# Block 1's second product as seven half products, with its inputs ahead of most of w2

## The chip, the core and the metric

The kernel runs on one core of one Trainium2 chip. TensorE (PE in the profile, its weight loads PEld) multiplies, VectorE (DVE), ScalarE (ACT) and GpSimd (POOL) do the rest, and SyncE (SP), POOL and ACT issue the transfers. Each engine takes its instructions in the order in which they were written. The metric is the device time of one execution in microseconds.

## What is computed

There are 8 batches of 576 rows, and 8 heads of 64. Per head, `kv = k^T v` and `out = q kv`. Each row of each head is divided by its root mean square and multiplied by `g_norm`. The heads side by side give `x` (576 rows of 512). The second part is a layer with a residual:

```
xn  = (x - mean(x)) / sqrt(var(x) + 1e-6) * g_ln
out = x + relu(xn @ w_ch1) @ w_ch2        # w_ch1: 512 x 2048, w_ch2: 2048 x 512
```

The kernel scales the rows by the reciprocal of the standard deviation (`rstd`) only when the second product is evicted, since that factor passes through the relu.

## The kernel before

**Blocks.** Rows are worked through in blocks of 512, in four tiles of 128: one block for each batch (0 to 7), and a last one, "rem", of the 64 rows that each batch has left. A block has a first product (`mm1`, line 665, matmuls of line 675, evicted with a relu by ACT at line 678 into `m1`) and a second product. The first product is made for 1, 2 or 4 tiles at a time (matmuls of 128, 256 or 512 columns): one tile at a time in blocks 0 and 1, two in block 2, four behind it.

**The second product.** Blocks 0 and 1 make it directly: 64 matmuls of 512 columns each (line 697), evicted by `finish` (lines 702 to 708) with one DVE instruction per tile, which scales by `rstd` and adds `x`. The blocks in `SEVEN` (line 481) cut the product into 2 x 2 quarters and make it with seven half-size products instead of eight (`mm2_seven`, lines 539 to 600): 7 x 16 matmuls of 256 columns (line 519). The price is sums: T1 to T4 of the quarters of w2, made once (lines 494 to 497, 1.2 us each on DVE), and S1 to S4 of the quarters of `m1`, made for each block by DVE (`row_sums`, lines 499 to 511) while the first product still runs. p1 to p7 are evicted by ACT (line 553) or DVE (line 558), and POOL makes the remaining additions (lines 570 to 592). In block 2 the order is p1, p4, p2, p5, p6, p7, p3.

**A tile of x.** `plan_tile` (line 451) sets out the steps. First: `o` (four matmuls, line 298), its squares on ACT (304), their sum on DVE (`red`, 375). Two slots later: the root on ACT (383), and on DVE the reciprocal, y, x, the mean and the centred rows xc (390 to 422). Then the turn of xc into `xT_blk`, which the first product reads: on PE in block 1 (429, copied by ACT at 431), and by a transposing DMA from SP (433) from block 2 on. The variance (415) can come later. `kv_of` (264) makes kv of a batch, 40 small matmuls on PE and two casts on ACT. q is turned by `turn_q_dma` (217): a DVE copy and one long transposing DMA on SP; for batch 1 by `q_start` (884) and `q_turns` (892), two of five parts on PE.

**The order of the work** is written out by hand. PE's stream of products counts ticks (`tick`, line 757): a first product has 16, a direct second product 16, the seven products 14. `at(slot, fn)` (line 748) puts work in front of the matmuls of a tick. A slot is written as 32 x block + r; where the block is in `SEVEN`, what lies in its second half is squeezed:

```python
        if r > 16 and i < len(blocks) and blocks[int(i)] in SEVEN:
            r = 16 + (r - 16) * 14 / 16
        s = sum(30 if x in SEVEN else 32 for x in blocks[:int(i)]) + r
```

So tick 32 is the start of block 1 and tick 48 that of its second product; block 2 begins at tick 64. Work of one tick goes to its engines in the order of the slots, and row sums go ahead of it.

**Loads.** All loads from DRAM are issued by POOL, in order, and cast to bf16 on the way: batch 0, w1, then lines 172 to 178 (w2 in five parts, with q, k, v of batch 1 between them), then one batch after the other (`load_batches`, line 100). The later ones wait behind a tiny copy (`gate`, line 105) of what must have landed first. There are two buffers for q, k and v.

Of the kernel before, what the change touches and what calls it, by code (L numbers as in the profile page):

```python
# [14 lines left out]
def kernel(  # L15
# [11 lines left out]
    nc = tc.nc  # L27
# [142 lines left out]
        nc.vector.memset(t, 0.0)  # L170

    load_w2(0, 4)
    load_w2(4, 8)
    for dst, src in ((q_in, q), (k_in, k), (v_in, v)):
        load(dst[1], src, 1)
    load_w2(8, 10)
    load_w2(10, 12)
    load_w2(12, nDe)
# [299 lines left out]

    SEVEN = {2, 3, 4, 5, 6, 7, "rem"}
    H2, C2 = nDe // 2, Dm // 2
    SPLIT = (0, 6, 12, nDe)
    SPLIT_2, TICKS_2 = (0, 12, nDe), ((0, 1, 4, 7), (0, 1, 4, 6))
# [5 lines left out]
    def w2_q(odd, cols):  # L490
        return w2_sb[:, odd::2, cols * C2:cols * C2 + C2]

    B11, B12, B21, B22 = (w2_q(o, c) for o, c in ((0, 0), (0, 1), (1, 0), (1, 1)))
    weight_sums = (lambda: nc.vector.tensor_sub(T1, B12, B11),
                   lambda: nc.vector.tensor_sub(T3, B22, B12),
                   lambda: nc.vector.tensor_add(T2, T3, B11),
                   lambda: nc.vector.tensor_sub(T4, B21, T2))

    def row_sums(b, i0, i1, ticks):
        if b not in sums:  # L500
# [38 lines left out]
    def mm2_seven(b):  # L539
        V, G = nc.vector, nc.gpsimd  # L540
        S1, S2, S3, S4 = sums.pop(b)
        a11, a12, a22 = m1_q(b, 0, 0), m1_q(b, 0, 1), m1_q(b, 1, 1)
        b11, b21, b22 = w2_q(0, 0), w2_q(1, 0), w2_q(1, 1)
        x, o, o_sb = outs(b)
        p_x, p_q = half(ps1, "p1", "p_x"), half(ps1, "p1", "p_q")
        p_y, p_z = half(ps2, "p2", "p_y"), half(ps2, "p2", "p_z")
        v0, v1, r5, u2, u3, q = (half(fpool, n, n) for n in ("v0", "v1", "r5", "u2", "u3", "q"))
        rstd = rstds[b]

        def scaled(dst, src, rows):  # L550

            for t in range(2):
                nc.scalar.activation(dst[:, t], src[:, t], func=AF.Copy,  # L553
                                     scale=rstd[:, 2 * rows + t:2 * rows + t + 1])

        def scaled_add(dst, src, rows, other):
            for t in range(2):
                V.scalar_tensor_tensor(dst[:, t], in0=src[:, t],  # L558
                                       scalar=rstd[:, 2 * rows + t:2 * rows + t + 1],
                                       in1=other[:, t], op0=ALU.mult, op1=ALU.add)  # L560

        def p1():
            product(p_x, a11, b11, True, False)
            scaled(v0, p_x, 0)
            scaled(v1, p_x, 1)

        def p2():
            product(p_x, a12, b21, False, True)
            scaled(o(0, 0), p_x, 0)
            G.tensor_add(o(0, 0), o(0, 0), x(0, 0))  # L570

        def p3():
            product(p_y, S3, T3, False, True)
            scaled_add(u3, p_y, 1, v1)
            G.tensor_add(o(1, 0), u3, q)
            G.tensor_add(o(1, 1), u3, r5)
            store(b, 2, o_sb[1])

        def p4():
            product(p_q, a22, T4, True, True)  # L580
            scaled(q, p_q, 1)
            G.tensor_add(q, q, x(1, 0))  # L582

        def p5():
            product(p_z, S1, T1, True, False)
            scaled(r5, p_z, 1)
            G.tensor_add(r5, r5, x(1, 1))

        def p6():
            product(p_y, S2, T2, True, False)  # L590
            scaled_add(u2, p_y, 0, v0)
            G.tensor_add(u2, u2, x(0, 1))

        def p7():
            product(p_z, S4, b22, False, True)
            scaled_add(o(0, 1), p_z, 0, u2)
            store(b, 0, o_sb[0])

        for p in ((p1, p4, p2, p5, p6, p7, p3) if b == 2 else (p1, p4, p6, p5, p2, p3, p7)):
            p()  # L600

    def mm2_seven_last(b):
# [62 lines left out]
    def mm1(b, t0, n, c0=0, c1=nDe):  # L665
# [3 lines left out]
        for de0 in range(c0, c1, per):  # L669
            tick()  # L670
            p1 = ps1.tile([128, per, n * 128], f32, tag="p1", name="p1")
            for i in range(per):
                de = de0 + i
                for kk in range(nK):
                    nc.tensor.matmul(p1[:, i, :], lhsT=w1_sb[:, kk, de * 128:(de + 1) * 128],  # L675
                                     rhs=blk[2][:, kk, sl],
                                     start=(kk == 0), stop=(kk == nK - 1))
            nc.scalar.activation(m1[:, de0:de0 + per, sl], p1, func=AF.Relu)  # L678
            del p1
            if b == 2 and t0 + n == 4 and de0 + per in SPLIT_2:  # L680
                i = SPLIT_2.index(de0 + per)
                row_sums(b, SPLIT_2[i - 1] // 2, SPLIT_2[i] // 2, TICKS_2[i - 1])
            elif b in SEVEN and b != 2 and de0 + 1 in SPLIT:
                i = SPLIT.index(de0 + 1)
                row_sums(b, SPLIT[i - 1] // 2, SPLIT[i] // 2, range(4))

# [15 lines left out]
    def finish(b, ts, p2):  # L702
        if ts % 2 == 0:
            o_pair[b] = outp.tile([128, 2, Dm], f32, tag="osb", name="o_sb")
        o_sb = o_pair[b][:, ts % 2]
        nc.vector.scalar_tensor_tensor(o_sb, in0=p2, scalar=rstds[b][:, ts:ts + 1],
                                       in1=blks[b][0][:, ts], op0=ALU.mult, op1=ALU.add)
        store(b, ts, o_pair[b][:, ts % 2:ts % 2 + 1])

    def store(b, ts, o_sb, c0=0, c1=Dm, upper=None):  # L710
# [163 lines left out]
    at(5, lambda: t[2].turn(True))  # L874
    at(5.1, before_5)
    at(9.5, next_memsets)
    load_batches(9.6, (("k", 2), ("v", 2), ("q", 2)), lambda: ())
    at(11, lambda: t[3].turn(True))
    for i in range(4):
        at(16 + i, lambda i=i: t[i].var())  # L880
# [13 lines left out]
        turn_q(1, 1, ps_m, "misc")  # L894
        del q_ps[1]

    at(14.5, q_start)
    at(19, q_turns)
    at(23, lambda: kv_of(1))
    for j, s, tn in ((0, 24, 30), (1, 27, 34), (2, 31, 38), (3, 35, 42)):  # L900
        plan_tile(s, lambda j=j: main_tile(1, j), tn, True, s + 6.7)
    at(36.2, lambda: keep_q(1))
    at(46, lambda: rstd_of(1))

    at(36, lambda: kv_of(2))
    at(36.9, lambda: turn_q_dma(2))
    for j, s, tn in ((0, 45, 51), (1, 49, 55), (2, 53, 61), (3, 57.5, 63)):
        plan_tile(s, lambda j=j: main_tile(2, j), tn, False, s + 6.7)
    at(58, lambda: keep_q(2))
    at(70, lambda: rstd_of(2))  # L910


    def turned_q(b):
        return (qts[b][:1, J, HP - 1, 127:] if b in qts else qj[:1, b, HP - 1, 63:])

    for slot, what, after in (
            (47, (("k", 3), ("v", 3), ("q", 3)), lambda: (turned_q(2),)),
            (68, (("q", 4), ("k", 4), ("v", 4)),
             lambda: (turned_q(3), blks[2][2][:1, nK - 1, 511:])),
            (92.7, (("q", 5), ("k", 5), ("v", 5)), lambda: (turned_q(4),)),  # L920
# [2 lines left out]
        load_batches(slot, what, after)  # L923


    for b, s in ((3, 56), (4, 93), (5, 123), (6, 155), (7, 187)):
        at(s, lambda b=b: kv_of(b))
    rems = {}

# [84 lines left out]
```

## Time and profile before

| what | value |
|---|---|
| median of 3 runs | 279.48 us (279.31 to 280.29) |
| the profiled execution | 279.33 us, span 277.3 us |
| PE busy | 269.2 us, 97% of the span, granted clock 1.0 |
| DVE, ACT, POOL busy | 195.9, 179.5, 101.7 us |
| block 0's second product starts on PE | 32.44 us |
| block 1's first product, second product | from 48.48 us, from 64.89 us |
| block 2's first product, second product | from 80.23 us, from 95.14 us |
| block 3 starts | 109.20 us |
| DMA engines | full from about 6 us to about 55 us, some 200 GB/s |
| last part of w2: issued, landed | 30.26 us, 43.67 us |
| q, k, v of batch 1 landed | 31.19, 34.11, 37.31 us |

The times in the rows are counted from the first instruction. The span is a little shorter than the execution's own time, which is the one that is compared. A view in order of time has the start, the length, the engine, the line, the operation, what it writes and reads, the count, and in square brackets the idle time ahead of it with what ended it. "Landed" is when the semaphore of a transfer showed it as complete.

### The profile page before, as it was taken

The page shows a single profiled execution, that of the slowest core. Times are in us where ns is not written, and L with a number is a line of the kernel's source. Part 1 is how long each engine was busy: PE and PEld are TensorE (multiplying, and loading weights), DVE is VectorE, ACT ScalarE, POOL GpSimd, SP SyncE. Part 2 cuts the span into 40 slices and gives each one's busy share as a digit, 9 for nine tenths or more (in the row PEclk, how much of TensorE's full clock was granted, in tenths as well). Part 3 has the DMA queues.
Part 4 walks back from the last instruction along what each step waited for, and adds up shares of the span by engine and source line. Part 5 has one row for each costly group of instructions (what it writes and reads, how often), then busy time and mean ns, then how long its engine had stood idle before and what let it go on. Part 6 is the DMA issues. An engine that isn't in the chain of part 4 may idle for free.

```text
span 277.3 us, 6629 instructions
## 1 busy us (share of the span) xinstructions
PE 269.2 (97%) x2614; PEld 189.6 (68%) x2614; DVE 195.9 (71%) x446; ACT 179.5 (65%) x398; POOL 101.7 (37%) x127
## 2 busy tenths in 40 slices
PE   8899999999999999999999999999999999999994
PEld 3589855996569886458845874597458745874683
DVE  6676438897966898899569856985797469923564
ACT  3567754796448783777677767776777487846610
POOL 8522770025034256701870187017201800180141
PEclk9999999999999999999999999999999999999999
DMA  7999999959995994995499639991611061105032
GB/s 215 199 207 205 200 197 190 260 106 144 189 183 84 199 126 92 216 227 98 41 185 239 134 26 178 245 134 21 161 28 21 20 163 29 21 20 151 2 76 76
DMA packets 65366, 36.80 MB, mean 133 GB/s; under 512 B 35120, under 2 KB 62004, under 8 KB 65336
## 3 DMA queue, kind: packets, MB, share of 16 engines
q0 software_dynamic: 28736, 18.29, 46.4%
q1 hardware_dynamic: 36008, 17.12, 30.4%
q10 hardware_dynamic: 592, 0.98, 1.0%
q8 instruction: 20, 0.33, 0.5%
q14 instruction: 10, 0.08, 0.1%
HBM read 36.71 MB, written 9.44 MB: 166 GB/s over the span
## 4 chain that ended last, share of the span: by engine, by line
PE 82%; DVE 8%; DMA 4%; ACT 3%; issue 1%; POOL 1%; DVEq 0%; POOLq 0%
PE p L675 42%; PE p L697 8%; PE p_y L519 7%; PE p_z L519 7%; PE p_x L519 6%; PE p_s L519 4%; DMA w_sb<-in_moe_w_ch_dram 4%; PE p_q L519 3%; PE o_ps L298 2%; PE kv_ps L271 2%; DVE S L509 1%; DVE ss L375 1%; DVE x_blk L397 1%; DVE o_ps L379 1%; DVE S L508 1%
## 5 line engine op out<-in xcount | busy, mean ns | idle before, releaser
L675 PE MATMUL p<-xT_blk,w_sb 128*128 128x128 bf16 (+2 forms) x1024 | 131.5, 286 | 0.6 <-DMA w_sb<-in_moe_w_ch_dram 0.4
L678 ACT ACTIVATE m<-p 128x512 bf16<-128x512 f32 x144 | 85.5, 597 | 38.9 <-PE p L675 36.2
L675 PEld LDWEIGHTS <-w_sb 128*128 128x128 bf16 x1024 | 78.7, 98 | 45.0 <-issue 0.7
L519 PEld LDWEIGHTS <-m 128*128 128x128 bf16 x448 | 43.3, 98 | 6.5
L375 DVE TENSOR_REDUCE ss<-sq 128x8 f32<-128x512 f32 x35 | 23.8, 680 | 28.7 <-ACT sq L304 28.6
L582 POOL TENSOR_TENSOR q<-q,x_blk 128x512 f32<-128x512 f32 x6 | 8.1, 1348 | 83.1 <-ACT q L553 83.1
L519 PEld LDWEIGHTS <-S 128*128 128x128 bf16 x344 | 32.8, 98 | 4.8 <-DVE S L509 1.1
L697 PE MATMUL p<-w_sb,m 128*128 128x512 bf16 x128 | 29.6, 379 | 0.0
L415 ACT ACTIVATE dev<-x_blk,st_blk 128x512 f32<-128x512 f32 x36 | 25.8, 718 | 1.4 <-DVE st_blk L401 1.4
L379 DVE TENSOR_TENSOR o_ps<-o_ps,inv 128x512 f32<-128x512 f32 x33 | 23.1, 700 | 3.1
L304 ACT ACTIVATE sq<-o_ps 128x512 f32<-128x512 f32 x35 | 20.8, 595 | 5.0 <-PE o_ps L298 5.0
L397 DVE SCALAR_TENSOR_TENSOR x_blk<-o_ps,g_norm_sb 128x512 f32<-128x512 f32 x33 | 22.8, 691 | 1.1
L519 PE MATMUL p_x<-w_sb,m 128*128 128x256 bf16 x192 | 23.4, 273 | 0.0
L697 PEld LDWEIGHTS <-m 128*128 128x128 bf16 x128 | 12.0, 98 | 12.3
L383 ACT ACTIVATE rms<-ss,eps_sb 128x8 f32<-128x8 f32 x36 | 10.7, 297 | 12.6 <-DVE ss L375 12.2
L507 DVE TENSOR_TENSOR S<-m 128x768 bf16<-128x768 bf16 (+2 forms) x20 | 10.7, 536 | 11.4 <-ACT m L678 11.4
L422 DVE TENSOR_SCALAR xc<-x_blk,st_blk 128x512 bf16<-128x512 f32 x32 | 17.7, 553 | 1.1
L558 DVE SCALAR_TENSOR_TENSOR u<-p_y,rstd,v 128x256 f32<-128x256 f32 x24 | 10.4, 476 | 5.0 <-PE p_y L519 5.0
L509 DVE TENSOR_TENSOR S<-m,S 128x768 bf16<-128x768 bf16 (+2 forms) x20 | 12.6, 634 | 0.4
L553 ACT ACTIVATE v<-p_x,rstd 128x256 f32<-128x256 f32 x24 | 9.4, 475 | 5.0 <-PE p_x L519 5.0
L390 DVE RECIPROCAL inv<-rms 128x8 f32<-128x8 f32 x36 | 7.1, 197 | 7.6 <-ACT rms L383 7.3
L519 PE MATMUL p_z<-w_sb,S 128*128 128x256 bf16 x96 | 11.8, 273 | 0.6 <-DVE S L509 0.6
(143 smaller groups left out, 347.6 us busy)
## 6 DMA issues: line engine op xcount, KB each, us to landing
out_dram<-o_sb SPq DMA_DIRECT2D x24, 256.0 KB, 6.1
w_sb<-in_moe_w_ch_dram POOLq DMA_DIRECT2D x7, 512.0 KB, 13.5
q_in<-in_q_dram POOLq DMA_DIRECT2D x7, 320.0 KB, 5.2
k_in<-in_k_dram POOLq DMA_DIRECT2D x7, 320.0 KB, 7.8
v_in<-in_v_dram POOLq DMA_DIRECT2D x7, 320.0 KB, 11.1
q_in<-in_q_dram POOLq DMA_DIRECT2D x8, 256.0 KB, 8.2
out_dram<-o_sb SPq DMA_DIRECT2D x16, 128.0 KB, 4.6
k_in<-in_k_dram POOLq DMA_DIRECT2D x7, 256.0 KB, 8.7
```

The costliest lines, as they stand in the source:

```text
L304: nc.scalar.activation(self.sq_t, self.o_ps, func=AF.Square)
L375: nc.vector.tensor_reduce(self.ss, self.sq_t, axis=AX.X, op=ALU.add)
L379: nc.vector.tensor_mul(self.o_ps, self.o_ps, self.inv().to_broadcast([128, H, D]))
L383: nc.scalar.activation(self.r, self.ss, func=AF.Sqrt, scale=1.0 / D, bias=eps_sb)
L397: nc.vector.scalar_tensor_tensor(x_blk[:, ts].rearrange("p (h d) -> p h d", h=H), in0=self.o_ps, scalar=1.0, in1=g_norm_sb.to_broadcast([1 ...
L415: nc.scalar.activation(dev, x_blk[:, ts], func=AF.Square, bias=st[:, 1, ts:ts + 1], accum_out=st[:, 2, ts:ts + 1])
L422: nc.vector.tensor_scalar_add(self.xc_t, x_blk[:, self.ts], st[:, 1, self.ts:self.ts + 1])
L509: lambda: nc.vector.tensor_sub(S4, a12, S2),
L519: nc.tensor.matmul(dst[:, t - ts[0], :c1 - c0], lhsT=a[:, i, t * 128:(t + 1) * 128], rhs=w[:, i, c0:c1], start=start and t == ts[0] and i ...
L675: nc.tensor.matmul(p1[:, i, :], lhsT=w1_sb[:, kk, de * 128:(de + 1) * 128], rhs=blk[2][:, kk, sl], start=(kk == 0), stop=(kk == nK - 1))
L678: nc.scalar.activation(m1[:, de0:de0 + per, sl], p1, func=AF.Relu)
L697: nc.tensor.matmul(p2[:, c0:c1], lhsT=m1s[b][:, de, ts * 128:(ts + 1) * 128], rhs=w2_sb[:, de, c0:c1], start=(de == 0), stop=(de == nDe - 1))
```

## The change

Block 1 joins `SEVEN`, so that it makes its second product with seven half products, in block 2's order. The block then has 30 ticks: block 2 begins at tick 62, and everything behind it counts two ticks less. What goes with it:

- The loads of q, k and v of batch 1 are issued ahead of w2's rows 4 to 8 (of 16), which are cut in two. Block 0's second product is cut to match.
- The weight sums are made in four pieces of two slices, the first at slot 13, and the rest at 34.5, 37 and 39.
- In blocks 1 and 2 three of POOL's additions (`o(0,0)`, `q`, `r5`) are put off until p6 has been evicted.
- `finish` of tiles 0 and 1 (block 0 alone uses it now) scales on ACT and adds on POOL.
- Block 1's first product is made for two tiles at a time.
- Batch 1's steps come two to four slots earlier. Batch 2's tiles, its kv and its q get new slots, some of which lie around the row sums of block 1, and so do those of batch 3. Batches 2 and 3 load q first.

```diff
     load_w2(0, 4)
-    load_w2(4, 8)
     for dst, src in ((q_in, q), (k_in, k), (v_in, v)):
         load(dst[1], src, 1)
+    load_w2(4, 6)
+    load_w2(6, 8)
     load_w2(8, 10)
...
-    SEVEN = {2, 3, 4, 5, 6, 7, "rem"}
+    SEVEN = {1, 2, 3, 4, 5, 6, 7, "rem"}
...
-    weight_sums = (lambda: nc.vector.tensor_sub(T1, B12, B11),
-                   lambda: nc.vector.tensor_sub(T3, B22, B12),
-                   lambda: nc.vector.tensor_add(T2, T3, B11),
-                   lambda: nc.vector.tensor_sub(T4, B21, T2))
+    def weight_sums(i0, i1):
+        i = slice(i0, i1)
+        t1, t2, t3, t4, b11, b12, b21, b22 = (w[:, i] for w in (T1, T2, T3, T4, B11, B12, B21, B22))
+        nc.vector.tensor_sub(t3, b22, b12)
+        nc.vector.tensor_add(t2, t3, b11)
+        nc.vector.tensor_sub(t4, b21, t2)
+        nc.vector.tensor_sub(t1, b12, b11)
...
+        late = []
+        def add(dst, a, c):
+            if b in (1, 2):
+                late.append(lambda: G.tensor_add(dst, a, c))
+            else:
+                G.tensor_add(dst, a, c)
...
-            G.tensor_add(o(0, 0), o(0, 0), x(0, 0))
+            add(o(0, 0), o(0, 0), x(0, 0))
...
-            G.tensor_add(q, q, x(1, 0))
+            add(q, q, x(1, 0))
...
-            G.tensor_add(r5, r5, x(1, 1))
+            add(r5, r5, x(1, 1))
...
             G.tensor_add(u2, u2, x(0, 1))
+            while late:
+                late.pop(1 if len(late) == 3 else 0)()
...
-        for p in ((p1, p4, p2, p5, p6, p7, p3) if b == 2 else (p1, p4, p6, p5, p2, p3, p7)):
+        for p in ((p1, p4, p2, p5, p6, p7, p3) if b in (1, 2) else (p1, p4, p6, p5, p2, p3, p7)):
...
-            if b == 2 and t0 + n == 4 and de0 + per in SPLIT_2:
+            if b in (1, 2) and t0 + n == 4 and de0 + per in SPLIT_2:
...
+        if ts < 2:
+            nc.scalar.activation(o_sb, p2, func=AF.Copy, scale=r)
+            nc.gpsimd.tensor_add(o_sb, o_sb, x)
+        else:
+            nc.vector.scalar_tensor_tensor(o_sb, in0=p2, scalar=r, in1=x,
+                                           op0=ALU.mult, op1=ALU.add)
...
-    load_batches(9.6, (("k", 2), ("v", 2), ("q", 2)), lambda: ())
+    load_batches(9.6, (("q", 2), ("k", 2), ("v", 2)), lambda: ())
...
-    at(14.5, q_start)
-    at(19, q_turns)
-    at(23, lambda: kv_of(1))
-    for j, s, tn in ((0, 24, 30), (1, 27, 34), (2, 31, 38), (3, 35, 42)):
-        plan_tile(s, lambda j=j: main_tile(1, j), tn, True, s + 6.7)
-    at(36.2, lambda: keep_q(1))
+    at(12.5, q_start)
+    at(17, q_turns)
+    at(20, lambda: kv_of(1))
+    for j, s, tn in ((0, 21, 27), (1, 24, 31), (2, 28, 35), (3, 31.5, 38)):
+        plan_tile(s, lambda j=j: main_tile(1, j), tn, True, (27.7, 33, 41, 44.5)[j])
+    at(33.2, lambda: keep_q(1))
...
-    at(36, lambda: kv_of(2))
-    at(36.9, lambda: turn_q_dma(2))
-    for j, s, tn in ((0, 45, 51), (1, 49, 55), (2, 53, 61), (3, 57.5, 63)):
-        plan_tile(s, lambda j=j: main_tile(2, j), tn, False, s + 6.7)
-    at(58, lambda: keep_q(2))
-    at(70, lambda: rstd_of(2))
+    at(40, lambda: kv_of(2))
+    at(34, lambda: turn_q_dma(2))
+    for j, s, tn in ((0, 43.2, 48), (1, 48.3, 53.5), (2, 58.3, 61.5), (3, 63.3, 67.5)):
+        plan_tile(s, lambda j=j: main_tile(2, j), tn, False, (55.5, 59.5, 63, 67.5)[j])
+    at(64, lambda: keep_q(2))
+    at(70.5, lambda: rstd_of(2))
...
-            (47, (("k", 3), ("v", 3), ("q", 3)), lambda: (turned_q(2),)),
+            (43, (("q", 3), ("k", 3), ("v", 3)), lambda: (turned_q(2),)),
...
-    for b, s in ((3, 56), (4, 93), (5, 123), (6, 155), (7, 187)):
+    for b, s in ((3, 60), (4, 93), (5, 123), (6, 155), (7, 187)):
...
-    for b, at_q, at_o in ((3, 56.2, (66.9, 70.7, 74.5, 78.4)), (4, 81, (96.5, 102.7, 109, 115)),
+    for b, at_q, at_o in ((3, 52.7, (68.5, 72.5, 76.5, 83)), (4, 81, (96.5, 102.7, 109, 115)),
...
-    for i, fn in enumerate(weight_sums):
-        at(40 + i, fn)
+    for i0, i1, slot in ((0, 2, 13), (2, 4, 34.5), (4, 6, 37), (6, 8, 39)):
+        at(slot, lambda i0=i0, i1=i1: weight_sums(i0, i1))
...
-    for de0, de1 in ((0, 8), (8, 10), (10, 12)):
+    for de0, de1 in ((0, 4), (4, 6), (6, 8), (8, 10), (10, 12)):
...
-    for ts in range(4):
-        mm1(1, ts, 1)
+    mm1(1, 0, 2)
+    mm1(1, 2, 2)
     mm2(1)
```

More of the change, by code (lines that the diff above doesn't have):

```diff
@@ L679, in mm1 @@
             del p1
-            if b == 2 and t0 + n == 4 and de0 + per in SPLIT_2:
+            if b in (1, 2) and t0 + n == 4 and de0 + per in SPLIT_2:
                 i = SPLIT_2.index(de0 + per)
                 row_sums(b, SPLIT_2[i - 1] // 2, SPLIT_2[i] // 2, TICKS_2[i - 1])
-            elif b in SEVEN and b != 2 and de0 + 1 in SPLIT:
+            elif b in SEVEN and b not in (1, 2) and de0 + 1 in SPLIT:
                 i = SPLIT.index(de0 + 1)
@@ L705, in finish @@
         o_sb = o_pair[b][:, ts % 2]
-        nc.vector.scalar_tensor_tensor(o_sb, in0=p2, scalar=rstds[b][:, ts:ts + 1],
-                                       in1=blks[b][0][:, ts], op0=ALU.mult, op1=ALU.add)
+        r, x = rstds[b][:, ts:ts + 1], blks[b][0][:, ts]
+        if ts < 2:
[4 more added lines that the diff above has]
+                                           op0=ALU.mult, op1=ALU.add)
         store(b, ts, o_pair[b][:, ts % 2:ts % 2 + 1])
```

## The prediction

> **What bounds the kernel now.** First the page's shares by engine, then the chain that ended last, then PE's waits, then DVE, ACT, POOL and SP in order of time between 28 and 110 us, then the DMA issues with their landings.
>
> ```profile
> PE 269.2 (97%) x2614; PEld 189.6 (68%) x2614; DVE 195.9 (71%) x446; ACT 179.5 (65%) x398; POOL 101.7 (37%) x127
> PEclk9999999999999999999999999999999999999999
> ```
>
> TensorE is busy 97% of the span at a full granted clock. What the other engines do counts only where TensorE waits for it. The chain gives the pace of each kind of product:
>
> ```profile
> 55.67 3.57 PE p L675 x64
> 66.14 3.45 PE p L697 x16
> 82.41 3.49 PE p L675 x32
> 123.85 1.75 PE p_x L519 x16
> ```
>
> The columns are start, length, line, count: 55.8 ns for 128 columns (first product, tile by tile), 215.7 for 512 (direct second product), 109.1 for 256 (first product by two tiles, 3.49/32) and 109.2 (seven-product form). Waits of PE:
>
> ```profile
> PE p L675 <- DMA w_sb<-in_moe_w_ch_dram: 0.4, 1, 0.4
> PE p_z L519 <- DVE S L509: 0.6, 1, 0.6
> ```
>
> Few are named, since most gaps are shorter than the list counts. I therefore add up PE's work from 32.44 us (block 0's second product starts) to 109.20 (block 3 starts), 76.76 us. Two direct second products 2 x 64 x 0.2157 = 27.60; the first product of block 1, 256 x 0.0558 = 14.28, and of block 2, 128 x 0.1091 = 13.97; the seven products of block 2, 7 x 1.747 = 12.23; turning q 0.45; four kv_of at 0.75 = 3.00; 16 groups of four matmuls (12 `o`, 4 turns) at 0.22 = 3.52. Sum 75.05, so 1.71 us are waits, about one of them in block 2's p7, where the lines below show why.
>
> ```profile
> 101.75 1.44 POOL L570 TENSOR_TENSOR o_sb<-o_sb,x_blk 128x512 f32<-128x512 f32 x1
> 101.99 3.42 DVE L509 TENSOR_TENSOR S<-m,S 128x1536 bf16<-128x1536 bf16 x2
> ```
>
> These are the timelines of POOL and DVE. The pair L509 takes 3.42 us, where a 128x1536 sum at 94.81 takes 0.95 and a 128x512 one 0.42: while POOL adds, such DVE instructions take turns with it.
>
> **The products.** Block 1's 64 matmuls of 13.80 us become 112 of 12.23: -1.57. Its first product by two tiles, 14.28 to 13.97: -0.31. No copies are added on PE. From block 3 on everything is PE-bound and unchanged, so what is won by 109 us is won at the end.
>
> [...]
>
> **The old waits.** At most 1.71 us go. Block 2's `q`, `o(0,0)` and `r5` adds now come after p6, so its S4 no longer alternates with them; and with finish(0) halved on DVE the rest of the small gaps may close. So the bound is 3.59 us (1.57 + 0.31 + 1.71), less whatever is late next.
>
> **Block 0, slots 12 to 31.** POOL's loads keep coming out of one full pipe, and the next is issued when an earlier one has landed:
>
> ```profile
> 30.26 0.76 POOL L119 DMA_DIRECT2D w_sb<-in_moe_w_ch_dram  x1 [1.11 <-DMA q_in<-in_q_dram]
> 33.66 4.37 SPq L888 DMA_TRANSPOSE qt<-q_p  x1
> ```
>
> Today w2(4,8) lands at 28.16, 2.5 us after w2(0,4), then q at 31.19, k at 34.11, v at 37.31, the last w2 at 43.67. Moved, q lands near 28.7 and v near 34.8; both halves of w2(4,8) follow. DVE copies q at 28.7 (0.82 as at 55.11, no memset on POOL yet, against 2.35 beside memsets), so SP issues L888 at 29.6, not 33.66. Landing 13.36 later as now: 43.0; bounds 4.9 (an undisturbed one, 56.09) and the old landing of 47.02. It moves 393 KB in 48 us summed over 16 engines, 3 us of the whole pipe, and now all of it lies ahead of the last w2: that comes 1.0 later, at 44.7. By adding PE's ticks: kv_of(1) at 36.4 needs v (35.1 with the transposition's share), w2(4,6) is needed at 37.1 (36.8), w2(6,8) at 39 (38.5), the rest of q at 44.7 (43.0), w2(12,16) at 45.0 (44.7). Nothing is late, by 0.3 at the closest. I take 0.1 for this and for tile 3's turn at tick 38, whose xc ends at 54.4 as PE arrives. The one extra DMA issue on POOL (0.75, w2(4,8) in two) hides in POOL's waits (1.1 to 1.9). The two finish(0) on ACT (0.6 each) and POOL (1.3 each) relieve DVE of 1.3; their stores leave some 1.5 later, and nobody waits. The sixteen small weight sums are 4 x 1.22 = 4.9 plus some 0.5 for the cut. A quarter runs at 29.5, where DVE waits for PE now, the rest by 59.4, ahead of p4 at 66.
>
> What stands behind the moved waits: behind the copy of q on DVE (slot 12.5) only the first weight sums and the scaling of w1, which waits for PE until 32.5 anyhow; behind `keep_q(1)` on POOL the gate copy of batch 3's loads, which itself waits for batch 2's q (its transposition issued at 55.1, landed near 60, as 60.95 now); behind the root of tile 3 on ACT (slot 33.5, free at 51.4 when its red is done) one eviction of the first product, due at 50.7 and done by 52.2, and PE, with three buffers, asks for that buffer at 52.6. Batch 2's loads end near 55.0 as now (55.03, the same bytes), with v in place of q as the last; kv_of(2) at slot 40 comes at 56.3. If that cover of 1.3 were gone, PE would wait one for one.
>
> **Batch 2's tiles and block 1's row sums.** T is the start of tick 43: 32.44 + 13.80 + 0.45 + 2 kv_of 1.50 + 8 groups 1.76 + 11 ticks of 0.873 = 59.6, with the 0.1 59.7. From T, PE reaches block 2's first half (tick 62) at 5 x 0.873 + 12.23 + 4 x 0.22 + 0.75 = 18.23. DVE, by its rows: red 1.15 to 1.75, second tile step 2.87 to 5.25 (82.14 to 87.38 in block 2 now), S1 and S2 of the first 12 (0.87 each) to 7.05, S1's rest 0.33, red of tile 1 0.60, S2's rest 0.33, S4 0.87 to 9.2, second step of tile 1 2.36 to 11.56, S4's rest 0.33, copy of q3 0.75 to 12.65. All sums precede their products (S1 at 10.1, S2 11.8, S4 13.8, S3 16.3). But SP first gets batch 3's q (slot 52.7), then tile 1's transposition (53.5):
>
> ```profile
> 76.92 3.17 SPq L224 DMA_TRANSPOSE qt<-q_p  x1
> 127.39 3.05 SPq L224 DMA_TRANSPOSE qt<-q_p  x1
> 130.49 3.38 SPq L433 DMA_TRANSPOSE xT_blk<-xc  x2
> ```
>
> q occupies SP for 3.1, so tile 1 is issued at T + 15.85. Such transpositions land after 2.4 to 8.6 us; 3.13 (131.96, no load or store beside it) is nearest, as batch 3's loads end near 74.5 and block 1's stores have not begun. Landed at T + 18.98: a new wait of 0.75.
>
> Then tile 3. Its `o` is at tick 61, T + 17.14. DVE is behind: S3 to 13.85, red 14.45, u2 15.3, tile 2's step from 15.7, whose xc waits for POOL's add and ends at 18.3; o(0,1) 19.15, red 19.75, u3 20.6. ACT's root stands behind the eviction of tick 62, at T + 20.7; tile 3's step starts at 21.0, its xc meets POOL's five adds (1.25 each, from 15.35) and is done at 23.8. Transposed:
>
> ```profile
> xT_blk<-xc SPq DMA_TRANSPOSE x1, 3.5
> ```
>
> That is the transposition of 80.14, beside block 1's stores as here; the next one took 4.00. T + 27.3. PE wants it at 18.98 + 8 x 0.873 + 0.22 = 26.2: another 1.1. Bounds of the two waits together: 0, and 6.2 at 8.6 us of landing. Block 2 behind it: batch 3's last tile is now at slot 83, its xc near 103, landed near 107 for 107.4; no wait, by 0.5.
>
> **Sum.** -3.59 + 0.1 + 0.75 + 1.1 = -1.6. The profiled execution took 279.33, its span 277.3; the median of the three is 279.48, 0.15 above. 279.33 - 1.6 + 0.15 = 277.9.
>
> **Rivals.** A, the forecast: 277.9, its own range 277.2 to 278.8 (landings of 2.4 to 4.4). B, the transpositions come in time: S sums and tiles run ahead of my DVE walk, since in the trace DVE has gaps of up to 3 us in this form of block (132.7 to 135.8); against it, SP's order is fixed. Then -3.5, 276.0. C, block 0 starves: the half of q that SP turns lands at the old 47.0 and PE waits 2.4 at tick 28, or w2 comes by as much later; for it, a pipe that is full from 4 to 55 us and margins of 0.3; against it, the bytes ahead of the last w2 are the same. 280.3. D, slower: tile 3's transposition, behind block 1's 512 KB store on the same SP queue and beside POOL's 512 KB, takes 7.5 to 8.6 as at 67.61, 91.44 and 116.70. 277.9 + 4.0 to 5.1, 281.9 to 283.0; the gain is gone at a landing of 5.1, and the kernel is slower by over 0.5% from 6.5. Against it: those three lay among POOL's loads, and batch 4's loads here wait for this very tile (the gate copy of line 105).
>
> **Chances.** A 0.44, B 0.25, C 0.16, D 0.15. About 0.5% (1.4 us, so 278.1 and 280.9) is what a measurement of this kernel can tell from no change. Of A 0.27 lies below 278.1 and 0.17 within; B is faster; of C 0.02 faster, 0.12 the same, 0.02 slower; of D 0.04 the same, 0.11 slower. Faster 0.54, same 0.33, slower 0.13. The range reaches to B and C, 276.0 to 280.3, and leaves out D's upper part and little of B.
>
> **What the profile after would show.** Sixteen matmuls of L519 in 1.75 us for block 1; L697 with 64 matmuls; block 1's second product starting near 64.4 and block 3 near 107.6, against 109.2. PE waiting for a DMA into xT_blk twice, near 78 and 86, 0.7 to 1.1 each; none for w2; none for S in block 2. The two finish steps on ACT near 46. A wait for w_sb or qt between 36 and 46 makes C right; a wait over 3 us at 86 makes D right.

## The result and the profile after

The changed kernel takes 283.66 us (median of 6 executions, 283.23 to 285.37), the kernel before 279.45 on the same chip. The ratio is 1.0154, with a 95% interval of 1.0127 to 1.0182: slower by 1.5%, where 277.9 was predicted and 276.0 to 280.3 was the range.

The profiled execution of the kernel after took 285.37 us, its span 283.4. It is the slowest of the six, for a reason that its clock row shows. These are the shares by engine and the granted clock, from the page of the kernel after:

```profile
PE 270.2 (95%) x2518; PEld 193.5 (68%) x2534; DVE 198.7 (70%) x466; ACT 184.6 (65%) x410; POOL 109.8 (39%) x134
PEclk9999999999999799999999999999999999999999
```

TensorE's share falls from 97% to 95%, and one slice in 40, near 95 us, has a granted clock of 0.7. PE's waits, in the same columns as before (who waits for whom, sum, times, longest):

```profile
PE p L690 <- DMA xT_blk<-xc: 2.7, 2, 2.0
PE o_ps L299 <- DMA qt<-q_p: 1.8, 1, 1.8
...
PE p L712 <- DMA w_sb<-in_moe_w_ch_dram: 0.8, 2, 0.4
PE p_y L523 <- DVE S L512: 0.6, 1, 0.6
```

The list counts idle time only. I count a wait as the distance from one matmul's start to the next, less the pace of its kind, which makes each 0.1 to 0.2 us longer. So counted, the kernel before has two waits of 0.15 us or more behind 30 us, 0.23 at 52.73 (`kv_of(2)`) and 0.74 at 105.47 (p7 for S), and the kernel after has seven. The chain that ended last passes through most of them (start, length, what):

```profile
30.71 15.32 DMA w_sb<-in_moe_w_ch_dram
...
56.45 6.59 DMA qt<-q_p
...
76.42 3.19 SPq L225
79.65 2.70 DMA xT_blk<-xc
82.39 1.05 PE p L690 x8
...
86.87 5.00 DMA xT_blk<-xc
92.01 5.32 PE p L690 x32
...
97.55 3.49 PE p L690 x32
```

| place | wait | PE waits for |
|---|---|---|
| 37.74 | 0.59 | w2's rows 4 to 6, landed 37.70 |
| 46.08 | 0.54 | w2's last rows, landed 46.03 (43.67 before) |
| 55.62 | 0.18 | xc of batch 1's tile 3 |
| 63.08 | 2.00 | batch 2's turned q, for `o` of its first tile |
| 82.39 | 0.84 | batch 2's tile 1 turned by SP |
| 92.01 | 2.18 | batch 2's tile 3 turned by SP |
| 133.76 | 0.72 | S of block 3, for its third product |

Together 7.05. The windows view shows what came with the last but one (window, us, PE busy, PEld, DVE, ACT, POOL, then granted clock, DMA share, GB/s):

```profile
90.00:92.00 2.00, 0.00 (x0) 0.03 (x1) 1.90 (x6) 0.88 (x2) 0.01 (x1) 1.00 0.48 117
92.00:94.00 2.00, 1.99 (x13) 1.54 (x14) 0.44 (x1) 0.60 (x1) 0.92 (x3) 0.66 0.33 66
94.00:96.00 2.00, 2.00 (x11) 1.44 (x10) 0.14 (x1) 0.79 (x2) 2.00 (x4) 0.50 0.62 52
```

After PE had stood still for 2.2 us the granted clock fell to half (at 92.64, 0.6 us after PE went on), and 32 matmuls of 256 columns took 5.32 us where the next 32 took 3.49. This cost 1.8 us in the profiled execution; the other five have a mean granted clock of 0.997 to 1.000, against 0.994.

The balance against the kernel before, in medians (the waits are those of the one profiled execution): +7.05 for the waits, -0.97 for the two old ones, -1.88 for the products. That is +4.20, and the medians differ by 4.21. For the profiled spans the clock's 1.8 comes on top; 283.4 - 277.3 is 6.1, which this sum meets within 0.1. Some of that agreement is luck. By the rows, the last block's first product starts 5.71 later (252.73 for 247.02), not 6.0, since gaps under 0.15 us each shrank too; and 0.4 more passes behind PE's last matmul (4.5 us instead of 4.1), where no wait was counted.

### The profile page after: what moved, and what is told of

It is laid out like the page before. It is cut to its first block, busy times and chain, and to the rows that moved or that the text cites. A ratio compares the mean times of both kernels' runs of the same rounds, so it can differ in the third digit from the quotient of the medians.

```text
span 283.4 us, 6487 instructions
## 1 busy us (share of the span) xinstructions
PE 270.2 (95%) x2518; PEld 193.5 (68%) x2534; DVE 198.7 (70%) x466; ACT 184.6 (65%) x410; POOL 109.8 (39%) x134
## 4 chain that ended last, share of the span: by engine, by line
PE 73%; DMA 20%; DVE 2%; SPq 1%; issue 1%; POOL 1%; ACT 1%; POOLq 0%
PE p L690 36%; DMA w_sb<-in_moe_w_ch_dram 9%; PE p_x L523 9%; PE p_z L523 8%; PE p_y L523 8%; DMA k_in<-in_k_dram 5%; PE p_s L523 4%; PE p_q L523 4%; DMA xT_blk<-xc 3%; DMA qt<-q_p 2%; PE o_ps L299 2%; PE p L712 1%; SPq L225 1%; PE kv_ps L272 1%; ACT v L557 1%
## 5 line engine op out<-in xcount | busy, mean ns | idle before, releaser
L690 PE MATMUL p<-xT_blk,w_sb 128*128 128x512 bf16 (+2 forms) x884 | 131.8, 305 | 3.9 <-DMA xT_blk<-xc 2.7
L523 PEld LDWEIGHTS <-m 128*128 128x128 bf16 x512 | 49.4, 98 | 7.2
L376 DVE TENSOR_REDUCE ss<-sq 128x8 f32<-128x512 f32 x35 | 23.8, 681 | 27.0 <-ACT sq L305 26.9
L523 PEld LDWEIGHTS <-S 128*128 128x128 bf16 x392 | 37.5, 98 | 5.1 <-DVE S L512 0.8
L523 PE MATMUL p_x<-w_sb,m 128*128 128x256 bf16 x224 | 27.3, 273 | 0.0
L605 POOL TENSOR_TENSOR u<-u,x_blk 128x512 f32<-128x512 f32 x7 | 8.9, 1266 | 37.0 <-DVE u L562 37.0
L511 DVE TENSOR_TENSOR S<-m 128x768 bf16<-128x768 bf16 (+2 forms) x22 | 12.5, 569 | 12.7 <-ACT m L693 12.7
L562 DVE SCALAR_TENSOR_TENSOR u<-p_y,rstd,v 128x256 f32<-128x256 f32 x28 | 12.2, 477 | 5.3 <-PE p_y L523 5.3
L712 PE MATMUL p<-w_sb,m 128*128 128x512 bf16 x61 | 15.0, 379 | 1.0 <-DMA w_sb<-in_moe_w_ch_dram 0.8
L523 PE MATMUL p_y<-T,S 128*128 128x256 bf16 x112 | 13.7, 273 | 0.6 <-DVE S L512 0.6
L523 PE MATMUL p_y<-T,m 128*128 128x256 bf16 x112 | 14.0, 272 | 0.0
```

The lines of the kernel that those rows point to most:

```text
L376: nc.vector.tensor_reduce(self.ss, self.sq_t, axis=AX.X, op=ALU.add)
L511: for i, fn in enumerate((lambda: nc.vector.tensor_add(S1, a21, a22), lambda: nc.vector.tensor_sub(S2, S1, a11), lambda: nc.vector.tensor_ ...
L523: nc.tensor.matmul(dst[:, t - ts[0], :c1 - c0], lhsT=a[:, i, t * 128:(t + 1) * 128], rhs=w[:, i, c0:c1], start=start and t == ts[0] and i ...
L712: nc.tensor.matmul(p2[:, c0:c1], lhsT=m1s[b][:, de, ts * 128:(ts + 1) * 128], rhs=w2_sb[:, de, c0:c1], start=(de == 0), stop=(de == nDe - 1))
```

## The experiments

Every kernel here does the whole computation; only its order or its way differs. Waits are counted as above. "e8" and so on stand for the labels below.

### The tile of the longest wait alone

```diff
-    for j, s, tn in ((0, 43.2, 48), (1, 48.3, 53.5), (2, 58.3, 61.5), (3, 63.3, 67.5)):
+    for j, s, tn in ((0, 46, 51), (1, 48.3, 53.5), (2, 58.3, 61.5), (3, 63.3, 67.5)):
```

> The changed kernel with one slot other: batch 2's first tile starts at slot 46 and not 43.2, so that its o comes behind the landing of batch 2's turned q (63.03 us there, when PE had come at 61.1). Theory W (the loss is a row of waits for single late transfers): the wait of 2.0 at that o is gone; the tile's DVE steps then run among the row sums, so the transposition of tile 1 comes about 1.4 earlier while PE comes 2.0 earlier, and the wait at block 2's start grows from 0.84 to about 1.4. 282.2 us (281.7 to 282.8) against 283.66. Rival R (one chain on DVE and SP, ending in tile 3's transposition, sets when block 2's second half starts, and a wait ahead of it is only its cover): no change, 283.3 to 283.7.

Measured: 285.43 us, ratio 1.0209 (1.0179 to 1.0240). Neither number came. The wait at 63 is gone, and another stands behind it, in PE's rows in order of time:

```profile
78.47 1.17 PE L272 MATMUL kv_ps<-v_in,k_in 128*64 128x64 bf16 x40 [2.53 <-DMA v_in<-in_v_dram]
79.57 3.13 PE L523 MATMUL p_z<-w_sb,S 128*128 128x256 bf16 x16
```

`kv_of(3)` waits 2.69 for batch 3's v, whose load stands behind the gate copy, which reads the same turned q (landed 63.83 here). So the late q had a second reader. To move one reader doesn't help; the transfer itself has to come earlier. The 16 matmuls behind it took 3.13 instead of 1.75: the clock fell here too (0.50 from 80 to 82 us).

### Batch 2's q turned earlier

Its DVE copy moves ahead of tile 3's steps of batch 1, which makes tile 3's turn a tick later.

```diff
-    for j, s, tn in ((0, 21, 27), (1, 24, 31), (2, 28, 35), (3, 31.5, 38)):
+    for j, s, tn in ((0, 21, 27), (1, 24, 31), (2, 28, 35), (3, 31.5, 39)):
...
-    at(34, lambda: turn_q_dma(2))
+    at(31.2, lambda: turn_q_dma(2))
```

> The changed kernel with batch 2's q copied and sent to SP's transposing DMA at slot 31.2 and not 34 (tile 3 of batch 1 turned at 39 and not 38, since its DVE steps now come behind that copy). Theory W2 (one late transposition, issued at 56.45 and landed at 63.03, makes PE wait 2.0 at batch 2's first o, and holds back batch 3's loads, which wait for it; that is why moving the o alone only moved the wait to kv_of(3)): issued near 53, landed near 60.5, no wait there and none at kv_of(3); the waits at ticks 62 and 70 stay: 281.7 us (281.2 to 282.3). Rival C (beside batch 2's last loads and block 0's stores it lands at 62.5 or later all the same): 283 or more.

Measured: 282.18 us, ratio 1.0101 (1.0085 to 1.0116), within the range. SP's queue in order of time, in the kernel after:

```profile
49.26 5.79 SPq L749 DMA_DIRECT2D out_dram<-o_sb  x8
56.45 3.08 SPq L225 DMA_TRANSPOSE qt<-q_p  x1
```

and in e8:

```profile
49.72 4.34 SPq L749 DMA_DIRECT2D out_dram<-o_sb  x6
54.24 3.66 SPq L225 DMA_TRANSPOSE qt<-q_p  x1
58.00 1.17 SPq L749 DMA_DIRECT2D out_dram<-o_sb  x2
```

The turn leaves 2.2 us earlier, between block 0's stores, and the 2.00 at 63 is gone with no new wait behind it. A new 0.53 appears at tick 38, where an eviction stands behind tile 3's root on ACT.

### Tiles 1 and 3 turned on PE

Four matmuls on PE and an ACT copy replace the two transfers that came late; batch 4's loads, which waited for tile 3's transfer, move from slot 68 to 71.5.

```diff
+    for j, s, tn in ((0, 43.2, 48), (1, 48.3, 62), (2, 58.3, 61.5), (3, 63.3, 71.3)):
+        plan_tile(s, lambda j=j: main_tile(2, j), tn, j in (1, 3), (55.5, 59.5, 63, 67.5)[j])
...
+            (71.5, (("q", 4), ("k", 4), ("v", 4)),
```

> The changed kernel with tiles 1 and 3 of batch 2 turned on PE (ticks 60 and 69, four matmuls and one ACT copy each) in place of SP's transposing DMA; batch 4's loads start 2.5 slots later, behind that turn. Theory W: the waits of 0.84 and 2.18 at ticks 62 and 70 are transfers and go, PE gets 2 x 0.22: -2.6, 281.1 us (280.6 to 281.6), and no drop of the granted clock behind the second wait. Rival S (what is late is xc itself, since DVE is loaded by block 1's sums): PE waits for xc at the turn, 283 or more.

Measured: 282.63 us, ratio 1.0120 (1.0094 to 1.0146), outside the range. The wait at tick 62 is gone, 0.46 of the one at tick 70 stays (now for the ACT copy), and the clock didn't fall. It is 1.5 short of the expectation, and half of that is one wait: `o` of batch 4 waits 0.79 for its turned q, since batch 4's loads and all behind them now come later.

### q, k and v behind w2's first half again

```diff
     load_w2(0, 4)
+    load_w2(4, 6)
+    load_w2(6, 8)
     for dst, src in ((q_in, q), (k_in, k), (v_in, v)):
         load(dst[1], src, 1)
-    load_w2(4, 6)
-    load_w2(6, 8)
```

> The changed kernel with the order of loads undone: both parts of w2's rows 4 to 8 again ahead of q, k, v of batch 1. Theory W: the two waits for w2 (0.59 and 0.54) go, but q, k and v land 2.5 later: kv_of(1) waits 0.9 for v, and the part of q that SP turns starts 2.5 later and lands at 46 to 47.5, so tile 2's o waits 1 to 2: 284.3 us (283.4 to 285). Rival L (the new order of loads is what costs): 281.5 to 282.5.

Measured: 285.08 us, ratio 1.0214 (1.0185 to 1.0244), just above theory W's range. The two waits for w2 (1.13) become 2.44 for q and v: 0.51 at the turns of q, 1.21 at `kv_of(1)`, 0.72 at an `o`. So the loads' order and the earlier steps of batch 1 belong together. Neither order feeds block 0 in time with those early steps.

### The seven products alone

The kernel before with block 1 in `SEVEN`, in block 2's order and with its row sums, and nothing else: old loads, old slots.

```diff
-    SEVEN = {2, 3, 4, 5, 6, 7, "rem"}
+    SEVEN = {1, 2, 3, 4, 5, 6, 7, "rem"}
...
+        for p in ((p1, p4, p2, p5, p6, p7, p3) if b in (1, 2) else (p1, p4, p6, p5, p2, p3, p7)):
...
+            if b in (1, 2) and t0 + n == 4 and de0 + per in SPLIT_2:
```

> The kernel before with one part of the change alone: block 1 makes its second product with seven half products, in block 2's order; loads, slots, weight sums, the first product one tile at a time and POOL's additions as before. Theory P (the seven products pay by themselves, the loss is made by the moves around them): -1.57, 277.9 us (277.4 to 278.4). Theory W (the sums on DVE and the shorter block make batch 2's tiles late without those moves too): tile 3's transposition lands at 88 to 90 us where PE comes at 86, a wait of 2 to 4, so 280 to 282.

Measured: 286.10 us, ratio 1.0232 (1.0202 to 1.0263), slower than the whole change and than either theory had it. The clock fell here too (mean 0.988 to 0.994 in all four executions), for 3.4 us of the profiled one (0.52 from 84 to 86 us), which costs it some 1.7. DVE can't do block 1's sums and batch 2's tiles in their old slots (timeline, DVE, ACT and PE; the brackets hold the idle time and its releaser):

```profile
73.68 2.35 DVE L509 TENSOR_TENSOR S<-m,S 128x1536 bf16<-128x1536 bf16 x2
75.95 0.67 DVE L375 TENSOR_REDUCE ss<-sq 128x8 f32<-128x512 f32 x1
...
76.66 0.30 ACT L383 ACTIVATE rms<-ss,eps_sb 128x8 f32<-128x8 f32 x1 [3.32 <-DVE ss L375]
...
79.20 1.91 PE L519 MATMUL p_z<-w_sb,S 128*128 128x256 bf16 x16 [3.47 <-ACT r L553]
...
83.15 1.03 PE L519 MATMUL p_y<-T,m 128*128 128x256 bf16 x8 [2.04 <-DVE u L558]
```

A tile's `red` stands behind the sums on DVE, ACT's root behind it, and the eviction that frees p_z behind the root: 3.64, then 2.20 for the next. So batch 2's tiles need other slots, and those of the change cure this. The two late transfers are their price as the change has them, but not a necessary one: e13 below keeps the first slot of each of these tiles, turns tiles 1 to 3 on PE and has neither wait.

### Block 1 direct again, all else as after

```diff
-    SEVEN = {1, 2, 3, 4, 5, 6, 7, "rem"}
+    SEVEN = {2, 3, 4, 5, 6, 7, "rem"}
```

(and the two conditions on row sums back to block 2 alone)

> The changed kernel with the seven half products alone undone: block 1 makes its second product directly, in 64 matmuls of 512 columns, without row sums; loads, slots, weight sums, additions and the first product by two tiles stay as changed. Theory W2: +1.57 of products, the waits for w2 (1.13) and batch 2's q (2.0) stay, those at ticks 62 and 70 (0.84 and 2.18) go with the sums and the two ticks more: 282.2 us (281.5 to 282.8). Rival S (the row sums and the extra evictions of block 1 carry the loss, the moves around them do not): 280 or less.

Measured: 282.60 us, ratio 1.0109 (1.0092 to 1.0126), within theory W2's range. The direct product takes 15.12 us (68.62 to 83.74 on PE), and the 3.02 of waits at ticks 62 and 70 are gone. What stays is 1.87 in block 0, 2.04 for batch 2's q, 0.90 in block 3. So 3.15 of the 4.21 us of loss stand without the seven products; the new order of loads, tiles and turns costs them. Of the 1.87, 0.57 is a wait at 46.00 for the part of batch 1's q that SP turns; e9 and e10, with the same loads, wait 0.69 each for it there, where the kernel after waits for w2.

### Taking the waits out, one after the other

e9 is e8 with tiles 1 and 3 on PE (slots 62 and 70.3) and batch 4's loads at slot 70, behind batch 3's q alone:

```diff
+    for j, s, tn in ((0, 43.2, 48), (1, 48.3, 62), (2, 58.3, 61.5), (3, 63.3, 70.3)):
+        plan_tile(s, lambda j=j: main_tile(2, j), tn, j in (1, 3), (55.5, 59.5, 63, 67.5)[j])
...
+            (70, (("q", 4), ("k", 4), ("v", 4)), lambda: (turned_q(3),)),
```

e10 puts batch 5's loads behind block 2's late adds:

```diff
-            (92.7, (("q", 5), ("k", 5), ("v", 5)), lambda: (turned_q(4),)),
+            (96.2, (("q", 5), ("k", 5), ("v", 5)), lambda: (turned_q(4),)),
```

e11 turns tile 2 on PE too (slot 65.5) and issues batch 4's loads ahead of block 1's late adds:

```diff
-            (70, (("q", 4), ("k", 4), ("v", 4)), lambda: (turned_q(3),)),
+            (63.4, (("q", 4), ("k", 4), ("v", 4)), lambda: (turned_q(3),)),
```

> The run with q early, and besides tiles 1 and 3 of batch 2 turned on PE (ticks 60 and 68), batch 4's loads at slot 70 waiting for batch 3's turned q alone. Theory W2: three waits of 2.0, 0.84 and 2.18 gone for 0.44 of PE: 279.1 us (278.5 to 279.8), level with the kernel before. Rival M (each wait that is taken away comes back in the next late transfer): 281 or more.

> The run before it, and batch 5's loads issued at slot 96.2 and not 92.7, so that POOL makes block 2's last two additions ahead of them, and not among block 3's row sums on DVE (there L513 took 1.50 us, and p6 of block 3 waited 0.72 for S). Theory W2: 0.6 to 0.7 less than the run before it, 278.4 us (277.8 to 279.1). Rival M: no less, since the loads come later and batch 5's q with them.

> The run with batch 5's loads behind the additions, and two edits more: batch 4's loads at slot 63.4 and not 70, so that POOL issues them ahead of block 1's last two additions and its store (there they began at 87.2 and ended at 104.9, among which batch 4's q took 9.5 us to turn and PE waited 0.79 for it), and tile 2 of batch 2 turned on PE too, since its transposition would meet these loads. Theory W2: 0.79 and the 0.28 behind it gone for 0.22 of PE: 279.6 us (279.0 to 280.3). Rival M: 280.5 or more, as the earlier loads make block 3's other transpositions late or keep DVE's row sums waiting.

Measured: e9 281.12 us, ratio 1.0053 (1.0033 to 1.0073), 2.0 short of what was expected and in the rival's range; e10 280.48, 1.0040 (1.0021 to 1.0059), the expected 0.6 below e9 but not the time, and the two intervals overlap; e11 280.20, 1.0022 (1.0001 to 1.0043), 0.3 below e10, within its range.

The three waits of 2.00, 0.84 and 2.18 are gone from e9. Of the 2.0 that is missing, its profiled execution shows half as waits that are new or have grown (0.45 for a tile of batch 3 at 108.99, and in block 0 and early in block 1 together 1.84 where the kernel after has 1.31). That execution is the fastest of the four (280.19); what makes the others 0.7 to 1.3 longer was not seen.

e10 settles the wait in block 3. DVE and POOL in order of time, in the kernel after:

```profile
122.03 0.95 DVE L512 TENSOR_TENSOR S<-S,m 128x768 bf16<-128x768 bf16 x1
123.02 1.50 DVE L513 TENSOR_TENSOR S<-m,S 128x768 bf16<-128x768 bf16 x1
...
120.29 0.73 POOL L98 DMA_DIRECT2D v_in<-in_v_dram  x1
120.97 1.59 POOL L588 TENSOR_TENSOR o_sb<-u,q 128x512 f32<-128x512 f32 x1
122.54 1.56 POOL L589 TENSOR_TENSOR o_sb<-u,r 128x512 f32<-128x512 f32 x1
```

Block 2's adds stand behind six load issues on POOL, so they fall on block 3's row sums, and both are slower: 1.59 and 1.56 us for the adds, 0.95 and 1.50 for the sums, where e10 has 1.26 and 1.27, 0.56 and 0.55. In e10, with the loads behind the adds, the same sums are alone, and the wait of 0.72 (0.79 in e9) is gone:

```profile
111.23 1.26 POOL L588 TENSOR_TENSOR o_sb<-u,q 128x512 f32<-128x512 f32 x1
...
121.89 0.56 DVE L512 TENSOR_TENSOR S<-S,m 128x768 bf16<-128x768 bf16 x1
...
123.26 0.55 DVE L513 TENSOR_TENSOR S<-m,S 128x768 bf16<-128x768 bf16 x1
```

The profiled e10 waits 0.79 elsewhere, at 109.36 for batch 4's turned q; e11 takes that out too. What is left in e11 of half a microsecond or more is 0.62 and 0.71 for w2 in block 0, and 0.53 at tick 38, early in block 1.

### Mending block 0 in two ways

e12 keeps the new order and tries to take these three out: w2's rows 4 to 6 ahead of v's second half, a third part of q turned on PE, `kv_of(1)` and tile 0 a tick later, batch 2's q copied at 32.5, and batch 0's variances and `rstd` later.

```diff
+        if src is v:
+            nc.gpsimd.dma_start(dst[1][:64], lo(src, 1))
+            load_w2(4, 6)
+            nc.gpsimd.dma_start(dst[1][64:, :, :J], up(src, 1))
...
+        turn_q(1, 2, ps_out, "ops")
...
+    at(21, lambda: kv_of(1))
...
+    at(32.5, lambda: turn_q_dma(2))
```

> The run before it, with block 0 eased besides: a third part of batch 1's q turned on PE (0.22), which takes 131 KB out of the transposition that runs against w2's loads; w2's rows 4 and 5 loaded ahead of the second half of v; kv_of(1) and tile 0 one tick later; block 0's last variances and its rstd behind the casts on ACT; batch 2's q copied at slot 32.5, between block 0's last finish and tile 3's second step. Theory W2: of the waits of 0.67, 0.69 and 0.53 in block 0 and at tick 38, 1.2 to 1.7 go: 278.3 us (277.8 to 279.2), below the kernel before. Rival M: 279.5 or more.

Measured: 280.73 us, ratio 1.0054 (1.0040 to 1.0068): missed, and in the rival's range. v's half now lands at 38.86, and `kv_of(1)` waits 1.65 for it:

```profile
39.11 0.82 PE L276 MATMUL kv_ps<-v_in,k_in 128*64 128x64 bf16 x40 [1.49 <-DMA v_in<-in_v_dram]
```

So each piece that was put ahead here made another late: with v ahead, w2's rows 4 to 6 landed at 37.70 and PE waited 0.59 for them (the kernel after); with these rows ahead of half of v, it waited 1.65 for v. e13 therefore goes back to the front of the kernel before (its loads, its slots for batch 1, one tile at a time in block 1's first product) and keeps e11's second half, with batch 2's q copied at 32.5:

```diff
     load_w2(0, 4)
+    load_w2(4, 8)
...
+    at(14.5, q_start)
+    at(19, q_turns)
+    at(23, lambda: kv_of(1))
+    for j, s, tn in ((0, 24, 30), (1, 27, 34), (2, 31, 38), (3, 35, 42)):
...
+    for i0, i1, slot in ((0, 2, 13), (2, 4, 13.5), (4, 6, 23.5), (6, 8, 39)):
```

> The kernel before up to the end of block 1's first product (its loads' order, its slots for the starts and turns of q and for batch 1's tiles, its weight sums, w2 waited for in the pieces 0 to 8, 8 to 10, 10 to 12, one tile of rows at a time in the first product), and behind that block 1's seven products with the second half of e11_loads_ahead_of_adds: batch 2's q turned earlier (its load first, its copy at tick 32.5), tiles 1 to 3 of batch 2 turned on PE, batch 4's loads at 63.4, batch 5's behind the late adds. Theory (the loss that is left in e11 lies in block 0, because q, k and v stand ahead of w2: waits of 0.62 and 0.71 for w2 and of 0.53 at tick 38): these three go (-1.9) and the first product by one tile at a time costs +0.3. Block 0's second product 16.0 as in the kernel before, block 3's first product starts near 107.2 to 107.9 instead of 109.45, and the time is 277.3 to 278.6, faster than before by 0.3 to 0.8%. Rival (batch 1's tiles, later by three ticks, push what follows): kv_of(3) waits for v3 near 73, or a tile of batch 2 for q2's transposition near 60, for 1 to 2 us: then 279.5 or more.

Measured: 279.73 us (12 executions, 278.94 to 280.99), ratio 1.0011 (0.9997 to 1.0026): as fast as before, not faster. The time is in the rival's range, without the rival's waits. The waits went as expected, from the waits view of e13 (the rows left out lie ahead of block 0's first product):

```profile
...
PE kv_ps L271 <- ACT xT_blk L431: 0.3, 1, 0.3
PE p_y L522 <- DVE u L561: 0.3, 1, 0.3
PE p L689 <- ACT xT_blk L351: 0.3, 1, 0.3
```

Block 3 starts on PE at 107.93 where it started at 109.43, so 1.5 is won by then. Of this 0.56 is lost again near 215 (a product waits for DVE, then a smaller one), 0.1 at the end, and 0.4 outside the span: the profiled execution took 278.94 for a span of 276.5, 2.44 around it, where the kernel before has 2.0. And the other eleven spans are 276.6 to 278.5. What makes them longer than the profiled one was not seen.

The last run undoes only the seven products in e13, with the same edit as in e4.

> e13_old_front with one thing undone: block 1 makes its second product directly, 32 groups of matmuls of 512 columns, without row sums (as in e4_direct). In a schedule in which PE waits nowhere for half a microsecond or more, this should show the seven products' own worth. Theory: the direct product takes 15.1 to 15.4 (15.12 in e4_direct) where the seven take 13.8 to 13.9, and nothing makes it up: block 2's first product starts at 80.6 to 80.9 instead of 79.31, and the time is e13's 279.73 plus 1.3 to 1.6, so 281.0 to 281.3 (by the span alone: 277.8 to 278.1 plus what lies around it). Rival: the order of batch 2's tiles and of the sums costs as much as the seven products save, so that without the sums DVE is earlier and waits go elsewhere: 280.3 or less.

Measured: 280.56 us, ratio 1.0042 (1.0028 to 1.0056). On PE block 1's second product takes 15.34 (65.76 to 81.10) against 13.82 in e13 (65.49 to 79.31): 1.52 is the seven products' own worth on PE, with the same other matmuls in both stretches. The median span is 1.3 longer than e13's, but the time only 0.83, because here 2.07 lies around the span and 2.44 in e13. The theory's product row came and its time (281.0 to 281.3) didn't. The rival's 280.3 didn't come either. But the two times don't differ by the products alone: the profiled e14 has waits that the profiled e13 hasn't, 0.47 at 60.84 for batch 2's turned q and 0.89 at 135.56 in block 3, and e13 has the two near 215 (0.47 and 0.21). So the 1.52 rests on PE's rows and not on the difference of the times.

## Why the prediction was wrong

| term of the sum | predicted | shown |
|---|---|---|
| block 1's products | -1.88 | -1.88 by the paces; -1.52 for the seven (e14) |
| old waits | -1.71 | -0.97 |
| block 0 and tile 3's turn at tick 38 | +0.1 | +1.31 |
| batch 2's q for its first tile | not in the sum | +2.00 |
| tile 1's transposition, tick 62 | +0.75 | +0.84 |
| tile 3's transposition, tick 70 | +1.1 | +2.18 |
| block 3 "unchanged" | 0 | +0.72 |
| sum | -1.64 | +4.20 |

**The products** were right. The seven use 1.75 us for each 16 matmuls of 256 columns, as forecast. The same block made directly, with the same old front, was slower: 15.34 us on PE for 13.82, and 280.56 (e14) for 279.73 (e13).

**The missing term.** The step that failed first is "batch 3's loads, which itself waits for batch 2's q (its transposition issued at 55.1, landed near 60 ...)". It counted this transfer for one reader, the gate, and not for `o` of batch 2's first tile at tick 43, which the same text puts at 59.7. By its own two numbers that was late already. And both ends were off. The copy on DVE stood behind tile 3's xc until 55.47, so the transfer was issued at 56.45:

```profile
55.07 0.49 DVE L423 TENSOR_SCALAR xc<-x_blk,st_blk 128x512 bf16<-128x512 f32 x1
55.47 0.82 DVE L223 COPY q_p<-q_in 128x2560 bf16<-128x2560 bf16 x1
```

And it took 6.59 to land, not 4.9. Why is open: block 0's last stores were still under way, but so they were in e12, where the same transfer, issued at 55.95, took 4.95. e8 issued it earlier, the wait was gone, and the time fell by 1.5 us of the 2.0 expected.

**Block 0.** "Nothing is late, by 0.3 at the closest. I take 0.1" failed by its margins. v was right (35.12 against 34.8 to 35.1), but w2's rows 4 to 6 landed at 37.70 for 36.8, and the last at 46.03 for 44.7. Rival C had the mechanism; its price of 2.4 was too high, since the two waits for w2 are 1.13. SP's turn of q landed at 45.21, 2.2 after my 43.0. PE didn't wait for it in this execution, but did by 0.57 to 0.69 in e4, e9 and e10, where it landed at 45.7 to 46.0. Between 36 and 38 us the transfers moved 133 GB/s where the windows on both sides have 198 and 196. The kernel before and e13 have no such stretch (205 and 206 between 36 and 38); e12, with the new order, has one of 87. That it comes with q's long turn running beside v's and w2's loads fits the time, but was not tested by itself.

**Tile 3 at tick 70** was mis-sized. It was issued where the prediction had it, 23.8 us after the start of tick 43 (63.08 to 86.87), but was to be done in 3.5, and took 5.00. My own threshold (the gain gone at 5.1) shows how close A and D lay. Tile 1's at tick 62 was right in cause, behind q3 on SP. That its size came too (0.84 for 0.75) is partly luck: it was issued 0.7 later than forecast, counted from tick 43, and landed 0.4 sooner.

**The old waits.** 1.71 came as a difference of two sums of 75 and 77 us. Gap by gap the rows give 0.97 in two waits; nearly all of the rest is gaps of under 0.15 us each, some 0.7 together, most of which stay. The wait of block 2's p7 for S, 0.74, went for the reason given: its last two sums now take 0.95 and 0.41 us (L513, at 105.47 and 106.94) instead of 3.42, and POOL makes no addition between 98 and 110 us.

**Block 3.** "From block 3 on everything is PE-bound and unchanged" failed: putting block 2's adds off moved them behind a run of load issues on POOL, onto block 3's row sums. The forecast followed these adds in block 2, where they helped, and not into the next block.

**The rivals.** They were given as one or the other. The waits lie at different places on one engine (97% busy before), and they added up (+4.20 in the balance with all seven, 4.21 measured): C's w2, part of D's tile, A's two, and q. D's bounds (281.9 to 283.0) come nearest to the outcome, for a cause that gave 1.1 of the 5.8 us by which the sum was off.

## What to carry to other kernels

When PE is busy 97% of the time, list for every moved transfer all of its readers with the time at which each needs it, and do the same for what stands behind it on its queue; a landing used once in the argument is easily forgotten for the other reader. Waits at different places on this engine added up in the balance (+4.20 for 4.21 measured, though taking three of them out gave 2.5 us in e9 and not 4.6), so the chance that none comes is small where there are six with margins of a few tenths. A saving in the engine's own work (here 1.5 us) was worth only what the other engines and queues could follow: seven products alone lost 6.6 us, the whole change 4.2, and with the old front and all but 1.2 us of the waits gone (e13) nothing was lost and nothing won.

## What was not expected of the hardware

**The clock after a short stop.** In the profiled executions, stops of PE of 1.65 (e12), 1.75 (e1), 1.85 (e8), 1.96 (e3), 2.00 (after), 2.01 (e5) and 2.04 us (e4) left the granted clock at 1.0. Stops of 2.18 (after), 2.24 (e5), 2.69 (e1) and 2.20 (e7) were each followed by a granted clock of 0.5 for some 3.4 us, 1.4 to 1.8 us lost: in the kernel after 18 matmuls of 256 columns ran in these 3.41 us (92.64 to 96.05), 32 of them and four of 128 in the next 3.41. The length of a stop doesn't decide alone: behind e7's stop of 3.64, which ended at 79.20, the clock stayed at 1.0 until 84.09, when the 2.20 had passed. In the clock records of the kernel after, the half clock lasts 3.413 us (from 92.64), and the full clock ahead of it and behind it 85.333 and 187.733, 25 and 55 times as long; in the kernel before the full clock lasts 273.066, 80 times. Counted in such steps from the first record of the full clock, the four falls come after 25, 26, 21 and 23 whole steps (in the kernel after 7.30 and 92.64), and each closes a step in which PE was busy for 1.40, 1.34, 0.88 and 1.38 us. Up to 270 us no other such step, in any of the fourteen traces, has PE busy for less than 1.48 (e7, 77.27 to 80.68); e4's stop of 2.04 left 1.54. So in these traces stops of 1.65 to 3.64 us cost 1.4 to 1.8 us by the clock or nothing, and the time that PE was busy in a step tells them apart. That is read from these four falls alone; no run was made to test it. The other executions of the kernel after kept a mean clock of 0.997 or more.

**Transpositions under load.** The same turn of q by SP landed 4.8 to 5.0 us after its issue in the kernel before and 5.0 to 6.6 in the kernel after, and a tile's after 2.4 to 8.5: 2.70 with stores yet to come, 5.00 with them beside. That the stores cause it was not tested.

**Time around the span.** It is nearly fixed for most kernels and differs between them: 1.89 to 1.97 for the kernel after, 1.95 to 2.08 before, 2.02 to 2.10 in e14, 2.39 to 2.52 in e13 (but 1.81 to 2.19 in e8 and 1.83 to 2.15 in e5). These 0.4 us are as much as what e13 won.
